# Transposed weight copies in pieces, the gradient of k inside the inverse loop, and weight-gradient jobs filled into layer 1's backward, in a forward-and-backward kernel of two SSM-convolution and MLP layers

## The chip, the cores and the metric

The kernel runs on one core of a Trainium2 chip. The metric is the device time of one execution in microseconds (us); the kernel before takes 758.16 us, the median of three runs (757.78 to 758.56). The profile is of one execution, with a span of 748.5 us.

## The reference

Forward pass of two equal layers on a sequence of S = 2048 tokens of width D = 448, all in bf16, and the gradients of its eight inputs for a given grad_out. B is one.

```
x = q
twice:  x = x + A(layernorm(x), k, v, shift_k, ssm_k, ssm_D)
        x = x + silu(layernorm(x) @ w1) @ w2           # w1: 448x1792, w2: 1792x448
A(q, ...) : k_shift[s] = sum over t < 4 of k[s - t] * shift_k[:, t]
            kv = k_shift * v
            y  = causal convolution of kv with ssm_k over the sequence (by FFT) + kv * ssm_D
            return q * y
outputs: x, and d/dq, d/dk, d/dv, d/dshift_k, d/dssm_k, d/dssm_D, d/dw1, d/dw2
```

The convolution result y doesn't depend on x, so it is computed once and used by both layers. d/dw1 and d/dw2 are sums over both layers and all tokens.

## The kernel before, in words

One core does everything in three parts.

**Prefix** (`_ssm_prefix`, to about 100 us): the shift convolution and the FFT convolution as matmuls against constant matrices. It leaves y in SBUF (`Ysb`) and the spectra in DRAM.

**Main** (`class Main`, about 100 to 512 us): the layers in chunks of 512 tokens (c = 0 to 3). The code counts L = 0 for the first layer and L = 1 for the second. The hidden width 1792 is NF = 14 blocks of 128, in two halves of seven. In the text, "layer 1" is L = 0 and "layer 2" is L = 1.

- `h` makes one half of the hidden activations: matmuls `ps_h` (L535, in `contract`), silu into `aT` on ScalarE, a copy `dT` for the slope. `out` multiplies with w2 (`ps_o`, L652). The program overlaps `h` of the next chunk with `out` of this one.
- `aT` and `ghT` tiles share the tag T with three buffers. Each half also has to be kept for the weight gradients, which contract over tokens and so need tokens on partitions: `store_turned` (L496) transposes the half by DMA into `turned` in two pieces and, at the next call, stores it to DRAM (`A_d` for activations, `GH_d` for hidden gradients, one for each layer). These transposes and stores are all issued by SyncE, in one queue.
- `load_weights_T` (L516) makes `w2T` and `w1T`, the transposed weights for the backward pass, by three DMA transposes straight from the inputs. It is called after chunks 1 and 2 of layer 1's forward.
- The backward of a chunk is `ga` and `gn`. `ga` makes the hidden gradient: matmuls `ps_g` with `w2T`, a ScalarE copy `ghp` (L679), a VectorE product with the slope into `ghT` (L687). `gn` multiplies with `w1T` (`ps_n`, L725) and goes back through both layernorms on VectorE and ScalarE (`ln_bwd`). `hook` inserts the slopes and the transposed gradient `gT` of the next chunk; `gT` goes through PSUM tag "tr", which has two banks.
- Layer 2's backward is interleaved with its forward; layer 1's backward runs by itself, about 410 to 512 us.

**Suffix** (`_ssm_suffix`, about 512 us to the end): the backward of the convolution, woven with the weight gradients. These are 56 jobs (`_job`, L864): load one transposed block `dstat` (128 x 16 x 128) from DRAM, and contract it with a moving tensor in 16 matmuls `ps_d` (L872). For each of 14 blocks `_gw2` runs two jobs (layer 1 with `X`, which holds the gradient into layer 2 by then, and layer 2 with `GO`, the loaded grad_out) and `_gw1` two (layer 2 with `mov3`, layer 1 with `mov1`, the normalised inputs). That is 896 matmuls in all. `dstat` has five slots once the suffix's own pool is open, three before. A gradient block of w1 is turned back by DMA (`turn`, L896) before its store. `weave(n)` puts the next n job matmuls between the suffix's own: after each block of the first FFT stage, the transposes, the spectra, the inverse, the gK blocks and the inverse loop `for i in range(8)` (L1076), which makes d/dv and `gks`. After that come the reduction for shift_k, then all remaining job matmuls, and in program order last `for g in range(8)` (L1127), which forms d/dk from `gks` with four products and three sums a group on VectorE.

What sets the order: the framework takes the instructions in program order as priority, places each on its engine's queue in an order that it simulates, and inserts the semaphores. An instruction whose inputs are there early can be placed ahead of others; `issue_after(i)` keeps what is traced in its block behind i on i's engine, and `keep_in_program_order(i)` holds an instruction at its place. [...]

Of the kernel before, what the change touches and what calls it, by code (L numbers as in the profile page):

```python
# [10 lines left out]
FP32 = mybir.dt.float32  # L11
# [109 lines left out]
def kernel(  # L121
# [38 lines left out]
    k.AP_d = dram.tile([4, P, S], BF16, name="AP_d")  # L160
    k.GH_d = [dram.tile([P, NF, NT, P], BF16, name=f"GH_d{i}") for i in range(2)]

# [318 lines left out]
class Main:  # L481

    def __init__(self, k, es):
        self.k, self.nc, self.tc = k, k.nc, k.tc
        nc, tc = k.nc, k.tc
        pool = lambda name, **kw: es.enter_context(tc.tile_pool(name=name, bufs=1, reuse_waits="tile", **kw))
        self.wt = pool("mwt")
        self.w2T = self.wt.tile([P, ND, F], BF16, name="w2T")
        self.w1T = self.wt.tile([P, NF, D], BF16, name="w1T")
        self.td = pool("mtd")  # L490
        self.ch = pool("mch")
        self.X = k.X
        self.late = None
        self.w1sb, self.w2sb, self.Y = k.w1sb, k.w2sb, k.Ysb

    def store_turned(self, dst, tile_, c, hh, groups=((0, 4), (4, 7))):  # L496
        nc = self.nc
        self.flush()
        an = self.td.tile([P, NF // 2, 4, P], BF16, name="turned", tag="S", bufs=2)
        for lo, hi in groups:  # L500
            nc.sync.dma_start_transpose(out=an[:, lo:hi].rearrange("p a t f -> p (a t) f"), in_=tile_[:, lo:hi, :].rearrange("p a s -> p (a s)"))
        lo, hi = groups[0][0], groups[-1][1]
        self.late = lambda: nc.sync.dma_start(out=dst[:, 7 * hh + lo:7 * hh + hi, 4 * c:4 * c + 4, :], in_=an[:, lo:hi])
# [6 lines left out]
    def turn_plain(self, i):  # L510
# [3 lines left out]
        self.late = lambda: self.nc.sync.dma_start(out=self.k.A_d[0][:, W2_PLAIN[i]], in_=an[:])  # L514

    def load_weights_T(self, which):  # L516
        nc, k = self.nc, self.k
        if which == 1:
            nc.sync.dma_start_transpose(out=self.w1T[:], in_=k.B_w1)
            return  # L520
        nc.sync.dma_start_transpose(out=self.w2T[:, 0:3, :], in_=k.B_w2[:, 0:384])
        nc.sync.dma_start_transpose(out=self.w2T[:, 3:4, :], in_=k.B_w2[:, 320:448])

# [147 lines left out]
    def ga(self, c, L, gT, dT, mid=None, loads=(None, None)):  # L671
        nc, k = self.nc, self.k
        ld = []
        ghT = [self.td.tile([P, NF // 2, 512], BF16, name=f"ghT{h}", tag="T", bufs=3) for h in range(2)]
        for fp in range(NF // 2):
            ps = k.psum.tile([P, 2, 512], FP32, name="ps_g", tag="mm", bufs=2)
            self.contract(ps, self.w2T, gT, 2 * fp, 2, None if fp == 6 else (fp + 1) % 2)
            gh = self.ch.tile([P, 2, 512], BF16, name="ghp", tag="ghp", bufs=2)
            k.last_gh = nc.scalar.copy(gh[:], ps[:])  # L679
            k.bal.add("act", 0.95)  # L680
            k.bal.add("dve", -0.5)
            if mid:
                with self.tc.issue_after(k.last_gh.ins):
                    mid(fp)
            for u in ((0, 1),) if fp != 3 else ((0,), (1,)):
                hh, o = divmod(2 * fp + u[0], 7)
                nc.vector.tensor_tensor(out=ghT[hh][:, o:o + len(u), :], in0=dT[hh][1][:, o:o + len(u), :], in1=gh[:, u[0]:u[0] + len(u), :], op=ALU.mult)  # L687
            k.bal.add("dve", 1.2)
            if fp in (3, 6):
                hh = (fp - 3) // 3  # L690
                if loads[hh]:
                    ld.append(self.load_d(*loads[hh]))
                self.store_turned(k.GH_d[L], ghT[hh], c, hh)
        return (ghT, *ld) if ld else ghT
# [20 lines left out]
    def gn(self, c, L, ghT, nb, gres, na, hook=None):  # L715
# [5 lines left out]
        for tl in range(4):  # L721
# [6 lines left out]
            k.bal.add("act", 0.75)  # L728
            k.pe_engine = mm.ins.engine
            if hook:  # L730
                hook(tl, mm.ins, last_u.ins)
# [35 lines left out]
    def run(self):  # L767
# [17 lines left out]
        for c in range(4):  # L785
# [7 lines left out]
            nT = self.b_tr(nb)  # L793
            if c in (1, 2):
                self.load_weights_T(3 - c)
            fol = []
# [3 lines left out]
        for c in range(4):  # L800
# [27 lines left out]
            self.gn(c, 1, ghT, nb, lambda tl: gb[:, tl, :], na, None if c < 3 else hook(0, d1))  # L828
            na, nb = na1, nb1
        for c in range(4):  # L830
            dT, (nb, na), (gb, gT) = ((None, d0), (None, d1)), nl, box.pop()
            ghT = self.ga(c, 0, gT, dT, (lambda fp: self.slope(e0, {1: (0,), 2: (1,), 4: (2,), 5: (3,)}.get(fp, ()))) if c < 3 else None, ((c + 1, 1) if c < 3 else None, (c + 2, 0) if c < 2 else None))
            if c < 3:
                d0, (ghT, d1, *e) = e0, ghT
                e0 = e[0] if e else None
            self.gn(c, 0, ghT, nb, lambda tl: self.X[:, 4 * c + tl, :], na, hook(c + 1, d1) if c < 3 else None)
            if c < 3:
# [26 lines left out]
def _job(k, ps, src, ft, mov, slot, start, stop, first=None):  # L864
    pl, tag, bufs = slot
    st = pl.tile([P, NT, P], BF16, name="dstat", tag=tag, bufs=bufs)
    with ExitStack() as es:
        if first is not None:
            es.enter_context(k.tc.issue_after(first))
        k.job_load = k.nc.sync.dma_start(out=st[:], in_=src[:, ft, :, :]).ins  # L870
    for t in range(NT):
# [17 lines left out]
def _gw1(k, pool, slots):  # L889
# [6 lines left out]
    def turn(ft, o):  # L896
        if ft < NF - 2:
            o7 = pool.tile([P, ND, P], BF16, name="do7", tag="do7", bufs=2)
            nc.sync.dma_start_transpose(out=o7[:, 0:3, :], in_=o[:, 0:384])
            nc.sync.dma_start_transpose(out=o7[:, 3:4, :], in_=o[:, 320:448])  # L900
            nc.gpsimd.dma_start(out=out7w[:, :, ft * P:(ft + 1) * P], in_=o7[:, 0:3, :])
            nc.gpsimd.dma_start(out=k.outs[7][384:448, ft * P:(ft + 1) * P], in_=o7[64:128, 3, :])
            return
# [8 lines left out]
    for ft in range(NF):  # L912
        ps = psum.tile([P, 512], FP32, name="ps_d", tag="tr", bufs=2)
        for L, mov in ((1, k.mov3), (0, mov1)):
            slot = slots.pop(0)
            slots.append(slot)
            for n, i in enumerate(_job(k, ps, k.GH_d[L], ft, mov, slot, L == 1, L == 0)):
                if hold and n == 7:
                    turn(*hold)
                    hold = None  # L920
                yield i
        o = pool.tile([P, D], BF16, name="dout", tag="dout", bufs=2)
        nc.scalar.copy(o[:], ps[:, :D])  # L923
        hold = (ft, o)
# [3 lines left out]
def _ssm_suffix(k):  # L928
# [7 lines left out]
    with ExitStack() as es:  # L936
# [6 lines left out]
        def jobs():  # L943
            yield from _gw2(k, k.dp, range(1), [(k.dp, "dstat", 3)], first=k.go_jobs.ins)
            yield from _gw2(k, k.dp, range(1, NF), both)
            yield from _gw1(k, dp2, both)
# [14 lines left out]
        for n2 in range(16):  # L961
            with _in_turn(k):
                _fft_stage1(k, n2, k.gYb[:, n2, :], A1, psum, nc.scalar if n2 < 12 else None)
            weave(4 if n2 < 12 else 12)
        with tc.tile_pool(name="sspec2", bufs=1, reuse_waits="tile") as p1:
# [105 lines left out]
        nc.gpsimd.dma_start(out=k.outs[6].rearrange("(o d) -> o d", o=1), in_=gD[:])  # L1071

        out3_pm = _pm(k.outs[3][0])
# [52 lines left out]
        weave(2 * NF * 2 * NT)  # L1126
        for g in range(8):  # L1127
            acc = p2.tile([P, 2, D], FP32, name="gk_acc", tag="gK", bufs=4)
            gk = p2.tile([P, 2, D], BF16, name="gk", tag="gk", bufs=2)
            last = None  # L1130
            for j in range(4):
                pj = p2.tile([P, 2, D], BF16, name="gkp", tag="gkv", bufs=2)
                for u, n in ((0, 2),) if 2 * g + j != J - 1 else ((0, 1), (1, 1)):
                    r = 2 * g + j + u
                    src = gks[:, r:r + n, :] if r < J else gkh[:, r - J:r - J + n, :]
                    nc.vector.tensor_tensor(out=pj[:, u:u + n, :], in0=src, in1=skb[:, j, :].unsqueeze(1).to_broadcast([P, n, D]), op=ALU.mult)
                if last is not None:
                    nc.vector.tensor_tensor(out=gk[:] if j == 3 else acc[:], in0=last[:], in1=pj[:], op=ALU.add)
                    last = acc
                else:  # L1140
                    last = pj
            nc.gpsimd.dma_start(out=out2_pm[:, 2 * g:2 * g + 2, :], in_=gk[:])

# [29 lines left out]
```

## Time and profile before

| what | value |
|---|---|
| time, three runs | 758.16 us (757.78 to 758.56) |
| span of the profile | 748.5 us |
| busy: TensorE / VectorE / ScalarE / GpSimd | 696.3 / 506.1 / 438.3 / 108.9 us |
| DMA | 184.88 MB moved, 247 GB/s mean |
| ps_d matmuls (all jobs) | 896, all of them in the suffix |
| turned<-ghT, transposes | 32, median 6.3 us from issue to landing |
| turned<-aT, transposes | 28, median 5.8 us |
| dstat<-GH_d, loads of 512 KB | 28, median 4.5 us |

TensorE is busy 93% of the span, so what counts is where it is not. In the lists of the profile a line gives the kernel line, the engine, the operation, and what is written from what. A releaser after an arrow is what ended a wait. "SPq" is SyncE's queue: the time of a row there is that of generating the transfer's descriptors, not of moving its bytes.

### The profile page before, as it was taken

Reading aid. Unit: us, or ns where it says so; the run is one execution under the profiler, and the core shown is the slowest. Engines: PE = TensorE matmul, PEld = TensorE weight load, DVE = VectorE, ACT = ScalarE, POOL = GpSimd, SP = SyncE. Lnnn points to the kernel's source line nnn. Section 1 sums busy time; section 2 is a strip of 40 time slices with the busy share of each in tenths; the row PEclk is TensorE's granted clock in tenths of the full one; section 3 lists DMA queues with packets and bytes.
Section 4 is the critical chain, followed back from the end, with each engine's and each line's share of the span. In section 5 each row is a group of like instructions: output and inputs, shape, how many; then the busy total and the mean of one; then the engine's idle time right before and its main releaser. Section 6 shows DMA issues by size and latency. Waiting matters only on the chain.

```text
span 748.5 us, 12463 instructions
## 1 busy us (share of the span) xinstructions
PE 696.3 (93%) x4836; PEld 370.4 (49%) x4881; DVE 506.1 (68%) x1059; ACT 438.3 (59%) x555; POOL 108.9 (15%) x180
## 2 busy tenths in 40 slices
PE   5988789599999999999999998989999999999997
PEld 5766533244444444443444334434556767555553
DVE  4878878468833398795966997899208773426970
ACT  4688767266636848688585787866325675410001
POOL 1143222022200000001000000000201112313321
PEclk9999999889999999999999999999999999999999
DMA  9979999999987889996989999999996976977993
GB/s 290 249 178 275 350 242 291 189 274 260 251 217 204 217 198 244 200 221 162 190 222 236 276 312 275 265 266 255 331 270 219 373 268 237 343 243 220 251 249 68
DMA packets 208343, 184.88 MB, mean 247 GB/s; under 512 B 155739, under 2 KB 184479, under 8 KB 207133
## 3 DMA queue, kind: packets, MB, share of 16 engines
q1 hardware_dynamic: 194272, 127.39, 68.9%
q0 software_dynamic: 13088, 54.18, 21.1%
q10 hardware_dynamic: 924, 2.52, 1.0%
q8 instruction: 38, 0.62, 0.4%
q14 instruction: 21, 0.16, 0.1%
HBM read 76.66 MB, written 65.87 MB: 190 GB/s over the span
## 4 chain that ended last, share of the span: by engine, by line
PE 53%; DVE 21%; ACT 10%; DMA 9%; issue 4%; POOL 1%; SPq 0%; DVEq 0%; ACTq 0%; POOLq 0%
PE ps_d L872 22%; PE ps_h L535 9%; PE ps_o L652 7%; DMA KB<-Z 3%; PE ps_n L725 3%; DVE lb_junk L700 3%; DMA turned<-aT 2%; PE ps_g L535 2%; DVE dT L113 2%; DVE lb_u L711 2%; DVE ghT L687 2%; PE ps_v L233 2%; PE ps_v L234 2%; DMA K_sb<-in_A_ssm_k_dram 2%; DVE lb_u L741 2%
## 5 line engine op out<-in xcount | busy, mean ns | idle before, releaser
L872 PEld LDWEIGHTS <-dstat 128*128 128x128 bf16 x896 | 85.5, 98 | 74.9 <-issue 0.2
L535 PE MATMUL ps_h<-nT,w1sb 128*128 128x512 bf16 (+1 forms) x432 | 103.9, 388 | 13.7 <-DVE dT L113 10.4
L535 PE MATMUL ps_g<-gT,w2T 128*128 128x512 bf16 (+1 forms) x432 | 93.3, 380 | 7.4 <-ACT ghp L679 6.0
L725 PE MATMUL ps_n<-w1T,ghT 128*128 128x448 bf16 x448 | 89.8, 353 | 2.8 <-DVE ghT L687 1.9
L627 ACT ACTIVATE aT<-ps_h 128x1024 bf16<-128x1024 f32 (+1 forms) x64 | 58.6, 917 | 56.0 <-PE ps_h L535 37.8
L652 PE MATMUL ps_o<-w2sb,aT 128*128 128x448 bf16 x448 | 91.3, 354 | 0.0
L872 PE MATMUL ps_d<-mov,dstat 128*128 128x448 bf16 x448 | 86.6, 352 | 0.0
L113 DVE CAST dT<-ps_h 128x1024 bf16<-128x1024 f32 (+1 forms) x55 | 58.4, 1064 | 40.8 <-ACT aT L627 40.7
L535 PEld LDWEIGHTS <-w1sb 128*128 128x128 bf16 (+1 forms) x448 | 36.5, 97 | 76.5 <-issue 49.2
L535 PEld LDWEIGHTS <-w2T 128*128 128x128 bf16 (+1 forms) x448 | 34.9, 97 | 65.5 <-issue 33.0
L679 ACT CAST ghp<-ps_g 128x1024 bf16<-128x1024 f32 x56 | 55.5, 1007 | 17.4 <-PE ps_g L535 12.7
L725 PEld LDWEIGHTS <-ghT 128*128 128x128 bf16 x448 | 42.3, 98 | 45.0 <-DVE ghT L687 5.1
L652 PEld LDWEIGHTS <-aT 128*128 128x128 bf16 x448 | 42.0, 98 | 42.8 <-issue 5.4
L923 ACT CAST dout<-ps_d 128x448 bf16<-128x448 f32 x14 | 7.5, 532 | 77.8 <-PE ps_d L872 77.8
L872 PE MATMUL ps_d<-GO,dstat 128*128 128x448 bf16 x224 | 49.7, 352 | 0.2
L872 PE MATMUL ps_d<-X,dstat 128*128 128x448 bf16 x224 | 49.6, 352 | 0.1
L727 ACT ACTIVATE lb_u<-ps_n,rstd 128x448 f32<-128x448 f32 x32 | 20.3, 636 | 31.1 <-DVE X L712 15.4
L234 PEld LDWEIGHTS <-pb 128*128 128x128 bf16 x336 | 32.5, 98 | 9.2 <-DVE pb L453 5.8
L233 PEld LDWEIGHTS <-pa 128*128 128x128 bf16 x336 | 32.8, 98 | 7.2 <-DVE pa L452 4.3
L687 DVE TENSOR_TENSOR ghT<-dT,ghp 128x1024 bf16<-128x1024 bf16 (+1 forms) x32 | 19.5, 620 | 20.9 <-ACT ghp L679 20.8
L612 ACT ACTIVATE dTl<-dTl 128x1024 bf16<-128x1024 bf16 (+1 forms) x32 | 29.8, 947 | 3.4 <-DMA dTl<-DT_d 3.4
L653 DVE TENSOR_TENSOR X<-X,ps_o 128x448 bf16<-128x448 bf16 x32 | 19.7, 617 | 15.3 <-PE ps_o L652 15.1
(205 smaller groups left out, 1170.0 us busy)
## 6 DMA issues: line engine op xcount, KB each, us to landing
GH_d<-turned SPq DMA_DIRECT2D x16, 896.0 KB, 4.9
dstat<-A_d SPq DMA_DIRECT2D x28, 512.0 KB, 5.7
dstat<-GH_d SPq DMA_DIRECT2D x28, 512.0 KB, 4.5
A_d<-turned SPq DMA_DIRECT2D x12, 896.0 KB, 5.1
DT_d<-dT POOLq DMA_DIRECT2D x8, 896.0 KB, 7.4
dTl<-DT_d SPq DMA_DIRECT2D x8, 896.0 KB, 6.1
spec_K<-Z POOLq DMA_DIRECT2D x7, 512.0 KB, 8.5
KB<-Z POOLq DMA_DIRECT2D x14, 256.0 KB, 12.1
```

What stands on the lines that cost most here:

```text
L113: eng.tensor_copy(out, in_)
L233: nc.tensor.matmul(o, lhsT=pa[:, i * P:(i + 1) * P], rhs=k.Gsb[:, ga, :], start=True, stop=False)
L234: nc.tensor.matmul(o, lhsT=pb[:, i * P:(i + 1) * P], rhs=k.Gsb[:, gb, :], start=False, stop=True)
L535: self.nc.tensor.matmul(ps[:, u, :], lhsT=w[lo:hi, b, f:f + P], rhs=x[lo:hi, b, :], start=(seen[u] == 1), stop=(seen[u] == ND))
L612: self.k.last_slope = self.nc.scalar.activation(s, s, ACT.Derivative_silu)
L627: last = nc.scalar.activation(a, ps[:, 0:n, :], ACT.Silu)
L652: nc.tensor.matmul(po[:, :D], lhsT=aT[ft // 7][0][:, ft % 7, tl * P:(tl + 1) * P], rhs=self.w2sb[:, ft, :], start=(ft == 0), stop=(ft == N ...
L679: k.last_gh = nc.scalar.copy(gh[:], ps[:])
L687: nc.vector.tensor_tensor(out=ghT[hh][:, o:o + len(u), :], in0=dT[hh][1][:, o:o + len(u), :], in1=gh[:, u[0]:u[0] + len(u), :], op=ALU.mult)
L700: nc.vector.scalar_tensor_tensor(out=junk[:], in0=u0, scalar=1.0, in1=n_t, op0=ALU.mult, op1=ALU.mult, accum_out=cp[:, 1:2])
L725: mm = nc.tensor.matmul(pn[:, :D], lhsT=ghT[ft // 7][:, ft % 7, tl * P:(tl + 1) * P], rhs=self.w1T[:, ft, :], start=(ft == 0), stop=(ft == ...
L872: i = k.nc.tensor.matmul(ps[:, :D], lhsT=st[:, t, :], rhs=mov[:, t, :], start=start and t == 0, stop=stop and t == NT - 1)
```

## The change

Four things are changed.

1. The transposed weights are fetched in six pieces instead of three transposes: after the third call of `store_turned`, each further call also issues one piece behind its own transposes, held at its place.
2. The first two blocks of `_gw2` (four jobs, 64 matmuls) can be consumed inside layer 1's backward: `fill(n)` takes up to n job matmuls and puts them behind TensorE's latest instruction, one or two after each group of `ps_g` (not in chunk 0) and two after each tile of `ps_n`. What is left of the two blocks is taken first in the suffix.
3. Layer 1's hidden gradient isn't transposed when it is made. GpSimd stores it plain (`GP_d`), and each layer-1 job of `_gw1` loads its block by a DMA transpose from DRAM. The gradient blocks of w1 are padded to 512 columns, so that `turn` needs one transpose instead of two.
4. d/dk: groups 0 to 5 are computed inside the inverse loop (`grad_k(i - 2)`), the last two after the jobs. To go with it, `weave` gives 4 instead of 12 matmuls in the last four FFT blocks, and 34 instead of 4 from the fourth turn of the inverse loop on.

```diff
@@ Main.__init__ / store_turned / load_weights_T
+        self.turns = 0
+        self.pieces = [(self.w2T[:, a:b, :], k.B_w2[:, lo:hi]) for a, b, lo, hi in ((0, 2, 0, 256), (2, 3, 256, 384), (3, 4, 320, 448))]
+        self.pieces += [(self.w1T[:, a:b, :], k.B_w1[:, a * P:b * P]) for a, b in ((0, 5), (5, 10), (10, NF))]
...
             nc.sync.dma_start_transpose(out=an[:, lo:hi].rearrange("p a t f -> p (a t) f"), in_=tile_[:, lo:hi, :].rearrange("p a s -> p (a s)"))
+        self.turns += 1
+        if self.turns > 3 and self.pieces:
+            out, src = self.pieces.pop(0)
+            i = nc.sync.dma_start_transpose(out=out, in_=src)
+            self.tc.keep_in_program_order(i)
...
-    def load_weights_T(self, which):
-        nc, k = self.nc, self.k
-        if which == 1:
-            nc.sync.dma_start_transpose(out=self.w1T[:], in_=k.B_w1)
-            return
-        nc.sync.dma_start_transpose(out=self.w2T[:, 0:3, :], in_=k.B_w2[:, 0:384])
-        nc.sync.dma_start_transpose(out=self.w2T[:, 3:4, :], in_=k.B_w2[:, 320:448])
...
-            if c in (1, 2):
-                self.load_weights_T(3 - c)
@@ Main.ga / gn
+            if L == 0:
+                self.fill(1 if fp else 2)
             k.last_gh = nc.scalar.copy(gh[:], ps[:])
...
-                self.store_turned(k.GH_d[L], ghT[hh], c, hh)
+                if L == 1:
+                    self.store_turned(k.GH_d, ghT[hh], c, hh)
+                else:
+                    self.flush()
+                    nc.gpsimd.dma_start(out=k.GP_d[7 * hh:7 * hh + 7, :, 512 * c:512 * (c + 1)].rearrange("ft f s -> f ft s"), in_=ghT[hh][:])
...
             k.pe_engine = mm.ins.engine
+            if L == 0:
+                self.fill(2)
@@ Main.run
+        k.jobs = _gw2(k, k.dp, range(2), [(k.dp, "dstat", 3)], first=k.go_jobs.ins)
+        bb = nc.cur_bb.bb
+
+        def fill(n):
+            last = next(i for i in reversed(bb.instructions) if i.engine == k.pe_engine)
+            with self.tc.issue_after(last):
+                for _ in zip(range(n), k.jobs):
+                    pass
+
         for c in range(4):
+            self.fill = (lambda n: None) if c == 0 else fill
...
+            self.fill = fill
             self.gn(c, 0, ghT, nb, lambda tl: self.X[:, 4 * c + tl, :], na, hook(c + 1, d1) if c < 3 else None)
@@ _job
-        k.job_load = k.nc.sync.dma_start(out=st[:], in_=src[:, ft, :, :]).ins
+        if src is None:
+            k.job_load = k.nc.sync.dma_start_transpose(out=st[:], in_=k.GP_d[ft]).ins
+        else:
+            k.job_load = k.nc.sync.dma_start(out=st[:], in_=src[:, ft, :, :]).ins
@@ _gw1
-            nc.sync.dma_start_transpose(out=o7[:, 0:3, :], in_=o[:, 0:384])
-            nc.sync.dma_start_transpose(out=o7[:, 3:4, :], in_=o[:, 320:448])
+            nc.sync.dma_start_transpose(out=o7[:], in_=o[:])
...
-            for n, i in enumerate(_job(k, ps, k.GH_d[L], ft, mov, slot, L == 1, L == 0)):
+            for n, i in enumerate(_job(k, ps, k.GH_d if L == 1 else None, ft, mov, slot, L == 1, L == 0)):
...
-        o = pool.tile([P, D], BF16, name="dout", tag="dout", bufs=2)
-        nc.scalar.copy(o[:], ps[:, :D])
+        o = pool.tile([P, 512], BF16, name="dout", tag="dout", bufs=2)
+        nc.gpsimd.memset(o[:, D:], 0.0)
+        nc.scalar.copy(o[:, :D], ps[:, :D])
@@ _ssm_suffix
-            yield from _gw2(k, k.dp, range(1), [(k.dp, "dstat", 3)], first=k.go_jobs.ins)
-            yield from _gw2(k, k.dp, range(1, NF), both)
+            yield from k.jobs
+            yield from _gw2(k, k.dp, range(2, NF), both)
...
-            weave(4 if n2 < 12 else 12)
+            weave(4)
...
+        def grad_k(g):
...
-            weave(4)
+            weave(4 if i < 3 else 34)
...
+            if i > 1:
+                grad_k(i - 2)
...
         weave(2 * NF * 2 * NT)
-        for g in range(8):
...
+        for g in range(6, 8):
+            grad_k(g)
```

`grad_k(g)` has the body of the old loop over g, unchanged.

More of the change, by code (lines that the diff above doesn't have):

```diff
@@ L160 @@
     k.AP_d = dram.tile([4, P, S], BF16, name="AP_d")
-    k.GH_d = [dram.tile([P, NF, NT, P], BF16, name=f"GH_d{i}") for i in range(2)]
+    k.GH_d = dram.tile([P, NF, NT, P], BF16, name="GH_d")
+    k.GP_d = dram.tile([NF, P, S], BF16, name="GP_d")
     bf = mybir.dt.np(BF16)
@@ L898, in turn @@
             o7 = pool.tile([P, ND, P], BF16, name="do7", tag="do7", bufs=2)
-            nc.sync.dma_start_transpose(out=o7[:, 0:3, :], in_=o[:, 0:384])
-            nc.sync.dma_start_transpose(out=o7[:, 3:4, :], in_=o[:, 320:448])
+            nc.sync.dma_start_transpose(out=o7[:], in_=o[:])
             nc.gpsimd.dma_start(out=out7w[:, :, ft * P:(ft + 1) * P], in_=o7[:, 0:3, :])
-            nc.gpsimd.dma_start(out=k.outs[7][384:448, ft * P:(ft + 1) * P], in_=o7[64:128, 3, :])
+            nc.gpsimd.dma_start(out=k.outs[7][384:448, ft * P:(ft + 1) * P], in_=o7[0:64, 3, :])
             return
@@ L1071, in _ssm_suffix @@
         nc.gpsimd.dma_start(out=k.outs[6].rearrange("(o d) -> o d", o=1), in_=gD[:])
+        def grad_k(g):
+            acc = p2.tile([P, 2, D], FP32, name="gk_acc", tag="gK", bufs=4)
+            gk = p2.tile([P, 2, D], BF16, name="gk", tag="gk", bufs=2)
+            last = None
+            for j in range(4):
+                pj = p2.tile([P, 2, D], BF16, name="gkp", tag="gkv", bufs=2)
+                for u, n in ((0, 2),) if 2 * g + j != J - 1 else ((0, 1), (1, 1)):
+                    r = 2 * g + j + u
+                    src = gks[:, r:r + n, :] if r < J else gkh[:, r - J:r - J + n, :]
+                    nc.vector.tensor_tensor(out=pj[:, u:u + n, :], in0=src, in1=skb[:, j, :].unsqueeze(1).to_broadcast([P, n, D]), op=ALU.mult)
+                if last is not None:
+                    nc.vector.tensor_tensor(out=gk[:] if j == 3 else acc[:], in0=last[:], in1=pj[:], op=ALU.add)
+                    last = acc
+                else:
+                    last = pj
+            nc.gpsimd.dma_start(out=out2_pm[:, 2 * g:2 * g + 2, :], in_=gk[:])
         out3_pm = _pm(k.outs[3][0])
@@ L1126, in _ssm_suffix @@
         weave(2 * NF * 2 * NT)
-        for g in range(8):
[L1128 to L1142, printed above, removed]
+        for g in range(6, 8):
+            grad_k(g)
 _INS = ['A_q', 'A_k', 'A_v', 'A_shift_k', 'A_ssm_k', 'A_ssm_D', 'B_x', 'B_w1', 'B_w2', 'grad_out']
```

## The prediction

> **What bounds the kernel now.** I read the page's slices first, then busy time by stage, then what ended TensorE's idle time in the stages where there is any.
>
> ```profile
> PE   5988789599999999999999998989999999999997
> DVE  4878878468833398795966997899208773426970
> PEclk9999999889999999999999999999999999999999
> ```
>
> Each digit is a fortieth of the span (18.7 us). TensorE is at 9 nearly everywhere after the prefix; the one hole is its 5 in slice 8 (131 to 150 us), with the granted clock at 8 beside it. Busy time by stage (TensorE, its weight loads, VectorE, ScalarE, GpSimd; then clock, DMA share, GB/s):
>
> ```profile
> 100.00:150.00 50.00, 37.38 (x185) 15.06 (x190) 33.23 (x79) 26.36 (x34) 10.10 (x14) 0.90 1.07 221
> 398.00:512.00 114.00, 105.43 (x564) 47.81 (x572) 100.02 (x274) 80.21 (x115) 2.17 (x4) 1.00 1.07 274
> 512.00:640.00 128.00, 126.81 (x1090) 81.19 (x1094) 66.69 (x130) 71.36 (x83) 20.38 (x36) 1.00 0.85 283
> 640.00:749.00 109.00, 103.86 (x774) 55.00 (x772) 57.06 (x93) 17.73 (x27) 28.29 (x48) 0.99 0.77 223
> ```
>
> The suffix (512 on) is TensorE itself: 1.2 us idle up to 640, then full until 744. Time can be won only from the 12.6 us idle in the first row and the 8.6 us in the second, since no matmul disappears. The hole, on TensorE and on SyncE's queue:
>
> ```profile
> 136.33 2.85 PE L535 MATMUL ps_h<-nT,w1sb 128*128 128x512 bf16 x11
> 148.44 3.29 PE L535 MATMUL ps_h<-nT,w1sb 64*128 64x512 bf16 x8 [9.26 <-DVE dT L113]
> ```
>
> ```profile
> 101.47 10.12 SPq L521 DMA_TRANSPOSE w2T<-in_B_w_dram  x1
> 111.64 2.45 SPq L522 DMA_TRANSPOSE w2T<-in_B_w_dram  x1
> 114.14 10.42 SPq L519 DMA_TRANSPOSE w1T<-in_B_w_dram  x1
> 124.66 13.19 SPq L501 DMA_TRANSPOSE turned<-aT  x2
> 147.02 0.38 SPq L503 DMA_DIRECT2D A_d<-turned  x1
> ```
>
> SyncE generates the weights' three transposes without a break from 101.5 to 124.6. The first turn of an activation tile aT queues behind them and lands at 147. ScalarE then waits 14.2 us "DMA turned<-aT" for that slot (tag T, three buffers), and TensorE stands for 9.26 us. In the second row TensorE's idle time is spread (410 to 512 us; after the bar: busy, mean ns, idle before and what ended it):
>
> ```profile
> L535 PE MATMUL ps_g<-gT,w2T 128*128 128x512 bf16 (+1 forms) x216 | 47.2, 380 | 5.7 <-ACT ghp L679 4.8
> L725 PE MATMUL ps_n<-w1T,ghT 128*128 128x448 bf16 x226 | 45.8, 353 | 2.8 <-DVE ghT L687 1.9 <-ACT lb_u L727 0.7
> ```
>
> 8.5 us in some twenty short waits for ScalarE and VectorE: room for matmuls that wait for neither.
>
> **What the Trainium skill says.** "Perfetto Trace Analysis", What "DMA-bound" means, lists the issuing sequencer as a bound of its own, solid slices being descriptor generation; the five rows above are that case. "TensorE: Matmul & The Clock Gate", HAM oscillation, says that a TensorE gap over about 3.4 us brings the throttle back. The trace agrees: the clock is 0.65 from 147 to 157 us, and in the backward of layer 1, whose gaps are at most 1.0 us, it is 1.00. "PSUM — Partial Sum Buffer", Engine vs sequencer instructions, has matmuls start in program order; so a filled job whose load is late stops everything behind it.
>
> **Part 1, weights in pieces.** Removed: three transposes with 23.0 us of issue ahead of the first turn. Added: the same bytes in six pieces, one behind each of turns 4 to 9, so 2.5 to 6.7 us each (10.12 us x 256/384 columns for the largest; 10.42 x 5/14 = 3.7 for one of w1T). Turns 1 to 3 have nothing ahead of them. Behind a piece in SyncE's queue stand the late store of that turn and the next turns. Between 150 and 235 us a half's two transposes and store take about 5 us of SyncE's time in some 18 us, so a piece fits; and aT comes round only after three halves, so several us more of landing reach nobody. The last piece follows turn 9 (about 228 to 233 us), and w1T is first read after 250. Gain: the 9.26 us, plus the cold restart. Eight ps_h matmuls took 3.29 us against 1.72 in "323.16 1.72 PE ps_h L535 x8" of the chain, sixteen transposes 1.91 against 1.06, five ps_o 1.46 against about 1.1: 2.7 us. Sum **12.0 us**. From 150 to 250 TensorE is busy 98.4 of 100 us, so nothing slower lies under the hole. Bounds 8 (another small wait in its place) and 12.5.
>
> **Part 2, w2 jobs filled in.** Fills: gn 4 chunks x 4 tiles x 2 = 32, ga 3 chunks x 8 = 24 (chunk 0 has none), 56 matmuls. A job of 16 takes 3.03 us in the chain (189 ns each): 10.6 us leave the TensorE-bound suffix and enter a stage with 8.5 us idle. If they displaced only busy time the gain would be 0; if they filled every hole, 8.5. Those in ga stand just where ps_g waits for ghp, those in gn where TensorE is ahead of VectorE anyway. I take 5. Their waits: dstat of the first jobs was loaded at 409.7, and X is complete when gn of layer 2 ends. GO is first read by fill 17, in gn of chunk 1 (about 447 us); it was issued at 438.6 and takes 8.6, and in the new kernel it has fewer transposes ahead of it. ps_d now holds one of the two "tr" banks, so a gradient's second transpose must wait for the copy of the first: three times up to 1 us, where the order has other matmuls to put between. Counted in the 5.
>
> **Part 3, layer 1's gradient unturned.** Sixteen SBUF transposes of ghT leave SyncE in 410 to 512, and GpSimd writes ghT plain. The same kind of store exists (AP_d<-aT, 5.7 us to landing, where a turn took 6.3), so ghT's slot is free no later: 0. Instead 14 loads become transposes out of DRAM in the last 100 us. The same form stands in the trace of before (the page has 5.6 us to landing for it; duration ns min/median/max here):
>
> ```profile
> L513 SPq DMA_TRANSPOSE turned<-AP_d x4: 2257/2418/2863, 230.4 to 288.8; - x4
> ```
>
> A load is issued when the job five before it ends, four jobs or 12.4 us ahead: hidden. SyncE's queue in one gw1 step of before:
>
> ```profile
> 701.81 1.20 SPq L899 DMA_TRANSPOSE do<-dout  x1
> 703.06 1.23 SPq L900 DMA_TRANSPOSE do<-dout  x1
> 704.39 3.19 SPq L870 DMA_DIRECT2D dstat<-GH_d  x2
> 707.87 1.46 SPq L899 DMA_TRANSPOSE do<-dout  x1
> ```
>
> A step is 6.06 us; SyncE's own work in it becomes one do transpose (1.2 to 2.5), one turned load (2.4) and one plain (0.4, the rest of the 3.19 being waits): 4.0 to 5.3 us. It holds, with little to spare. The padding memset on GpSimd is one small instruction per step, behind stores that end well within the step: 0.
>
> **Part 4, gradient of k in the loop; weaves 4 for 12 and 34 for 4.** One group costs VectorE four products and three sums:
>
> ```profile
> L1136 DVE TENSOR_TENSOR gkp<-gks,skb 128x896 bf16<-128x896 bf16 (+1 forms) x30 | 17.1, 605 | 2.4 <-DMA out_dram<-gsk 2.2
> L1138 DVE TENSOR_TENSOR gk_acc<-gkp 128x896 f32<-128x896 bf16 x8 | 8.7, 1092 | 0.3
> ```
>
> 4 x 0.605 + 3 x 1.09 = 5.7 us, with the loop's own two products (0.6 each) 6.9 us a turn. TensorE has 34 x 0.189 + 4 x 0.19 = 7.2 us a turn: VectorE stays just ahead, and ScalarE's gkv copy, which now shares its two buffers with the products, has the last product and sum (1.7 us) to pass in. Before, these groups lay under 67 us of jobs, so moving them gains nothing by itself. It keeps them off the end: jobs left after the shift reductions are 896 - 56 - 666 = 174 (33 us) instead of 348. The cost is in mov1: its load needs X, which gw2 now gives up in the middle of the gK section, and it is first read 33 matmuls later. By the counts that is about 11.8 us with the gK blocks between, against 9.4 us for the load: 0 to 3 us of stall. For this and for dense loads in the loop (DMA share 0.96 in 640 to 660 already) I take **1.5 us** loss.
>
> **Sum.** 758.2 - 12.0 - 5.0 + 1.5 = 742.7; I say 742.5.
>
> **Rivals.** (a) The fills only displace busy matmuls, or the transposes on one bank give it back: 758.2 - 12.0 + 1.5 = 747.7. For: VectorE is busy 91 of 102 us there. Against: the waits are on single copies, which a matmul in between covers. 0.20. (b) Everything hides: 758.2 - 12.0 - 8.5 = 737.7. For: TensorE ran dense through 640 to 740. Against: a fill cannot meet every wait in a fixed order. 0.12. (c) The pieces hold up later turns, and half of the hole opens again around 165 to 200 us: 742.5 + 6 to 10 = about 750. For: DMA share is about 1.0 there. Against: three halves of slack. 0.10. (d) The other side: turned loads cost SyncE as much in the last stage as the turns of ghT did under load. Sixteen of those took 68 us of issue from 416 to 512 (4.25 us for 448 KB, so 4.9 for 512 KB). A step is then 4.9 + 0.4 + 2 = 7.3 us against 6.06, 14 x 1.3 = 18 us, and 742.5 + 18 = 760.5. For: the kind is the same. Against: the AP_d row read from DRAM at 2.4 us. 0.08. The forecast has 0.50.
>
> **Range.** 737 to 753 holds the forecast, (a), (b) and (c); out are (d) and a tenth for a bound missed. Faster 0.89, within 0.2% 0.03, slower 0.08.
>
> **What would show it.** No TensorE gap over 2 us and clock near 1.0 from 100 to 250 us (part 1). In layer 1's backward, TensorE idle down from 8.5 to about 3 us, the stage about 5.5 us longer, with 56 ps_d matmuls in it (part 2). No ghT turn in it, and turned loads of 2 to 3 us issue later, TensorE dense from there to the end (part 3). gkp and gk_acc inside the inverse loop with no TensorE wait on gkv, and at most 3 us before the first matmul on mov1 (part 4). The prediction is wrong if ps_d waits for dstat, GO or mov1, or if aT still waits for a turn.

## The result, and the profile after

The changed kernel takes 747.5 us (median of four runs, 738.98 to 755.04) against 758.36 us for the kernel before (four runs, 757.78 to 759.94). By executions within 1.5% of the fastest of their kernel alone, the ratio is 0.975 (95% interval 0.9721 to 0.978); since one and the same kernel here differs by more than that through a wait of its own, which the experiments below show, medians and means over all executions are used from here on.

The predicted time was 742.5 us, in a range of 737 to 753. The four executions are two pairs, 739.0 and 740.4 us, 754.6 and 755.0 us; the median stands between them, where no execution was. The profiled execution has a span of 753.2 us. The slices of its page that answer to those shown of before:

```profile
PE   6988789999569999999999999999999999999997
DVE  4878878788423379696785997797516776299150
PEclk9999989999879999999999999999999999999999
```

The hole hasn't gone. It has moved from slice 8 to slices 11 and 12, 188 to 226 us, and the clock dips with it (0.54 of full speed from 200 to 210 us). Here is the timeline of TensorE around it in the kernel after:

```profile
196.34 1.79 PE L536 MATMUL ps_h<-nT,w1sb 64*128 64x512 bf16 x8
212.98 3.26 PE L536 MATMUL ps_h<-nT,w1sb 128*128 128x512 bf16 x8 [14.85 <-DVE dT L113]
```

SyncE's queue ahead of it (start, duration of the row):

```profile
165.88 10.12 SPq L505 DMA_TRANSPOSE turned<-aT  x2
176.04 10.44 SPq L509 DMA_TRANSPOSE w2T<-in_B_w_dram  x1
187.21 19.36 SPq L505 DMA_TRANSPOSE turned<-aT  x1
206.62 3.51 SPq L509 DMA_TRANSPOSE w2T<-in_B_w_dram  x1
```

A single turn of aT took 19.4 us of issue and the piece before it, a quarter of w2T, 10.4 us. ScalarE waited 15.7 us for that turn. In another execution of the same program, profiled in the experiments (span 740.3 us), the same four entries read:

```profile
157.23 8.16 SPq L505 DMA_TRANSPOSE turned<-aT  x2
165.43 2.42 SPq L509 DMA_TRANSPOSE w2T<-in_B_w_dram  x1
170.31 4.09 SPq L505 DMA_TRANSPOSE turned<-aT  x1
174.45 4.07 SPq L509 DMA_TRANSPOSE w2T<-in_B_w_dram  x1
```

and TensorE has no gap over 0.5 us between 106 and 300 us. The same instructions in the same order can cost 0 or 15 us.

The time of a row in SyncE's queue therefore isn't that of generating descriptors alone, as it was described ahead. The rows of w1T's transpose in the kernel before (114.14 us in its first profile, 111.97 in the second, shown below) take 10.42 and 19.39 us, and transpose packets of 1.64 and 1.58 MB begin in them; w1T is 1.61 MB. In these rows SyncE's queue goes on only at the pace at which the packets move.

Busy time by stage in that second execution: layer 1's forward up to the first ps_g, layer 2, layer 1's backward, the suffix up to the gK blocks, the rest (columns as in the table of stages in the prediction).

```profile
105.10:228.30 123.20, 120.46 (x630) 53.28 (x640) 86.59 (x176) 79.65 (x98) 22.75 (x30) 1.00 1.04 262
228.30:399.30 171.00, 165.25 (x883) 74.53 (x897) 125.42 (x276) 121.28 (x156) 7.17 (x10) 1.00 0.86 211
399.30:508.50 109.20, 104.65 (x545) 47.06 (x551) 93.40 (x257) 74.84 (x106) 10.65 (x15) 1.00 0.65 227
508.50:620.30 111.80, 109.85 (x929) 69.74 (x934) 66.20 (x126) 63.83 (x73) 18.45 (x32) 1.00 0.79 261
620.30:740.30 120.00, 111.06 (x878) 60.95 (x876) 57.80 (x94) 24.02 (x34) 31.52 (x62) 1.00 0.98 226
```

For the first profile of before the same five stages are 135.7, 171.0, 101.8, 116.8 and 119.7 us. The first stage is 12.5 us shorter. Layer 1's backward is 7.4 us longer, for 10.6 us of jobs moved into it. Suffix and end together are only 4.7 us shorter, where those jobs' 10.6 us are missing. So in these two traces parts 2 to 4 cost 2.7 us on balance. (The prefix, which wasn't changed, is 1.6 us longer in the second.)

### The profile page after: what moved, and what is told of

The parts are those of the page before. It is cut to its first block, busy times and chain, and to the rows that moved or that the text cites. A ratio compares the mean times of both kernels' runs of the same rounds, so it can differ in the third digit from the quotient of the medians.

```text
span 753.2 us, 12492 instructions
## 1 busy us (share of the span) xinstructions
PE 701.6 (93%) x4881; PEld 370.2 (49%) x4881; DVE 508.4 (67%) x1059; ACT 438.3 (58%) x555; POOL 118.4 (16%) x202
## 4 chain that ended last, share of the span: by engine, by line
PE 56%; DVE 20%; ACT 10%; DMA 8%; issue 4%; POOL 1%; SPq 0%; ACTq 0%; DVEq 0%; POOLq 0%
PE ps_d L893 20%; PE ps_h L536 9%; PE ps_o L653 7%; PE ps_g L536 5%; PE ps_n L732 4%; DMA KB<-Z 3%; DMA turned<-aT 3%; DVE lb_junk L707 3%; DVE lb_u L718 2%; DVE dT L113 2%; ACT nb L280 2%; PE ps_v L234 2%; PE ps_v L235 2%; DMA K_sb<-in_A_ssm_k_dram 2%; DVE lb_u L750 1%
## 5 line engine op out<-in xcount | busy, mean ns | idle before, releaser
L536 PE MATMUL ps_h<-nT,w1sb 128*128 128x512 bf16 (+1 forms) x448 | 106.9, 393 | 18.1 <-DVE dT L113 16.4
L536 PE MATMUL ps_g<-gT,w2T 128*128 128x512 bf16 (+1 forms) x448 | 96.0, 381 | 3.2 <-ACT ghp L682 2.7
L893 PE MATMUL ps_d<-X,dstat 128*128 128x448 bf16 x224 | 53.2, 353 | 0.0
L893 PE MATMUL ps_d<-GO,dstat 128*128 128x448 bf16 x224 | 51.7, 353 | 0.0
## 6 DMA issues: line engine op xcount, KB each, us to landing
GP_d<-ghT POOLq DMA_DIRECT2D x8, 896.0 KB, 10.1
```

Source lines behind the costliest of these rows:

```text
L536: self.nc.tensor.matmul(ps[:, u, :], lhsT=w[lo:hi, b, f:f + P], rhs=x[lo:hi, b, :], start=(seen[u] == 1), stop=(seen[u] == ND))
L893: i = k.nc.tensor.matmul(ps[:, :D], lhsT=st[:, t, :], rhs=mov[:, t, :], start=start and t == 0, stop=stop and t == NT - 1)
```

## The experiments

The runs are in three batches, each on one chip, with the kernel before beside them: 39, 7 and 75 executions of it.

### One size of hole, or many?

Theory A: the hole has a fixed size, set by what stands ahead in SyncE's queue. Theory B: the transposes are slowed by what else the DMA engines carry, so the size varies. Both kernels ran again unchanged.

> The kernel before, unchanged, profiled a second time. In its first profile TensorE stood 9.26 us at 139 us behind a late turn of aT, and that profile's span (748.5 us) was about 7 us under what the timed runs (758 us) would give. Theory A (the hole has one size, set by the 23 us of weight transposes ahead in SyncE's queue): again 9 to 10 us. Theory B (the turns and weight transposes are slowed by whatever else the DMA engines carry at that moment, so that the hole varies from execution to execution): another size, perhaps 16 us, with the same instructions everywhere else.

> The changed kernel, unchanged, profiled again. Its first profile had a hole of 14.85 us at 198 us behind a turn that took 19.4 us to issue. Theory A (pieces remove the wait, the first profile was a disturbed execution): no hole over 2 us before 250 us, 738 to 740 us. Theory B (the forward of layer 1 is close to what the transposing DMA can do beside the stores of GpSimd, so a late turn comes and goes): a hole of some other size, and timed runs in two groups about 15 us apart.

The kernel before, beside these runs: 735.4 to 775.7 us in 39 executions, median 752.0; in four more, one of them profiled, 752.5 to 760.8. Its new profile shows the hole in the same place, nearly twice as long as the first time (timeline of TensorE):

```profile
134.94 2.85 PE L535 MATMUL ps_h<-nT,w1sb 128*128 128x512 bf16 x11
155.51 3.29 PE L535 MATMUL ps_h<-nT,w1sb 64*128 64x512 bf16 x8 [17.71 <-DVE dT L113]
```

and on SyncE w1T's transpose took 19.4 us where it had taken 10.4:

```profile
111.97 19.39 SPq L519 DMA_TRANSPOSE w1T<-in_B_w_dram  x1
131.46 20.63 SPq L501 DMA_TRANSPOSE turned<-aT  x2
```

The changed kernel: 735.5 to 754.8 us in 12 executions, median 742.7. Eight are at 743.5 or below, four at 751 or above. The size varies, as theory B has it; whether its cause is the right one, these two runs don't show.

### Part 1 alone, and everything but part 1

```diff
 # part 1 alone: the kernel before, and
+        self.turns += 1
+        if self.turns > 3 and self.pieces: ...
-            if c in (1, 2):
-                self.load_weights_T(3 - c)
...
 # all but part 1: the changed kernel with these lines the other way round
```

> The kernel before with part 1 alone: weights in six pieces behind turns 4 to 9, nothing else changed. If part 1 carries most of the gain, as predicted (12.0 us of 15.5): about 12 us or more under before, 741 to 746 us. If the fills carry it: within 5 us of before.

> The changed kernel with the weights' three transposes as before: parts 2 to 4 without part 1. Predicted 5.0 - 1.5 = 3.5 us under before, about 754.5 us; the two traces so far show 1.9 us from the start of layer 1's backward to the end (TensorE's last matmul 6.5 us later at the start of it and 4.6 us later at the end), so 756 us. If the pieces are worth little: about 742 us.

Part 1 alone: median 740.0 us (20 executions, 735.7 to 755.6), 12.0 below the kernel before in the same batch (10.1 by the means, within 4.4, twice the standard error). All but part 1: median 751.4 (12 executions, 738.2 to 761.8), 0.6 below it. So part 1 carries the gain. It is a gain in how often and how long the hole appears, not in the best time: the fastest executions are 735.4 us (before), 735.5 (changed) and 735.7 (part 1 alone), and six of the 20 are still at 746.7 or above. The profiled execution of part 1 alone has a hole of 2.70 us, that of all but part 1 one of 4.34 us.

### What makes a transpose late

Three changes to the kernel before, with one suspect altered in each. With plain loads the backward multiplies with untransposed weights, so that its gradients are not those of the reference; the bytes are as many.

```diff
 # plain loads in place of the weights' transposes
-            nc.sync.dma_start_transpose(out=self.w1T[:], in_=k.B_w1)
+            nc.sync.dma_start(out=self.w1T[:], in_=k.B_w2.rearrange("(c p) d -> p c d", p=P))
...
 # stores on SyncE (or, in the third, on ScalarE: nc.scalar)
-            nc.gpsimd.dma_start(out=k.DT_d[c, half], in_=dT[:])
+            nc.sync.dma_start(out=k.DT_d[c, half], in_=dT[:])
...
-                nc.gpsimd.dma_start(out=k.AP_d[:, :, 512 * c:512 * (c + 1)]...
+                nc.sync.dma_start(out=k.AP_d[:, :, 512 * c:512 * (c + 1)]...
```

> The kernel before, with the three weight transposes replaced by plain loads of as many bytes into the same tiles, at the same place in the queue (so the backward multiplies with untransposed weights and the gradients are not those of the reference; no work is left out). The kernel before has a hole of 0 to 25 us behind the first turn of aT, and 735 to 776 us over its executions on this chip. Theory A (the transposes of the weights, ahead in the queue and slow beside other transfers, make the hole): no hole in the forward of layer 1, all executions at 735 to 739 us. Theory B (the turns of aT are slowed by the stores of GpSimd whatever is in front): the scatter stays, a median of 745 us or more.

> The kernel before, with the stores of dT and of the plain part of aT in layer 1's forward issued by SyncE, in the queue of the transposes, in place of GpSimd. Theory A (weights alone are to blame): hole and scatter as before, median about 752 us. Theory C (transposes are slow because packets of GpSimd's queue and of SyncE's alternate on the DMA engines): packets of one queue only, the transposes at about 20 ns a packet again, no hole, 735 to 740 us. If SyncE's own order gets in the way: a hole of a fixed size.

> The same stores issued by ScalarE, so a third hardware queue and not GpSimd's software queue. Theory C (any second queue's packets between the transposes make them slow): hole and scatter as before, about 752 us. Theory D (it is the software queue[...] that makes engines stand): no hole, 735 to 741 us. ScalarE gets eight or twelve issues of some 0.5 us, so up to 2 us more where it is the bound.

| kernel | executions | median us | range us |
|---|---|---|---|
| before, in this batch | 7 | 757.5 | 750.4 to 766.5 |
| plain weight loads | 4 | 738.8 | 735.7 to 745.1 |
| stores on SyncE | 4 | 741.0 | 740.5 to 741.5 |
| stores on ScalarE | 4 | 748.1 | 744.0 to 755.8 |

Without the weights' transposes the large hole goes; some scatter remains, against the expectation. With the stores in the transposes' own queue it goes too, as theory C has it, although the three weight transposes are still ahead. Their rows are then 8.72, 3.49 and 7.18 us long (10.12, 2.45 and 10.42 in the first profile of before), and the first turn lands in time:

```profile
112.98 7.18 SPq L519 DMA_TRANSPOSE w1T<-in_B_w_dram  x1
120.26 3.68 SPq L501 DMA_TRANSPOSE turned<-aT  x1
124.05 0.52 SPq L638 DMA_DIRECT2D DT_d<-dT  x1
124.66 2.83 SPq L501 DMA_TRANSPOSE turned<-aT  x1
```

With the stores in ScalarE's queue, which the profile lists as hardware_dynamic where GpSimd's is software_dynamic, the hole is there, though smaller (2.42 us in the profiled execution, the fastest of the four; a scatter of 12 us). So in these runs the long hole comes only with both: the weights' transposes queued ahead of the turn, and these stores in another queue beside them. It isn't a matter of GpSimd's software queue alone (theory D).

The packets show the slowing. I counted the 256-byte packets of SyncE's transposes from 100 to 240 us, in stretches of 1 us with and without packets of 512 bytes and more of another queue under way, as KB moved a microsecond in the stretches that had any. "Alone" means without another queue; SyncE's own plain packets stand in some of these stretches:

```
                          beside another queue   alone    hole in that execution
before, first profile              83             167         9.26 us
before, again                      68             164        17.71
after, first profile               50             169        14.85
after, again                      101             175         none
part 1 alone                       69             169         2.70
all but part 1                     78             163         4.34
stores on SyncE                    92             167         none over 1.1
stores on ScalarE                  80             163         2.42
plain weight loads                 78             161         none over 1.1
```

Alone, transposes move 161 to 175 KB/us in every execution. Beside another queue they move 50 to 101, and this number differs between executions of the same program. It doesn't by itself give the size of the hole: 68 KB/us goes with 17.71 us, and 69 with 2.70. The single packet's mean goes from 21 to 25 ns alone to 26 to 49 ns beside; single ones of 1 us and more are among both.

A rival is that the stores merely take their share of the DMA engines. On average they do: in the stretches beside another queue all queues together move 204 to 278 KB/us, and in the others 191 to 218. But in the wait itself both queues are slow. From 184 to 196 us of the first profile of after, the transposes move 27 and the other queues 50 KB/us, with packets of 136 and 805 ns in the mean. In the row of w1T's transpose in the first profile of before (114.14 to 124.56 us), which also has other queues' packets beside it, they move 158 and 121 KB/us, with packets of 23 and 284 ns. So sharing alone doesn't make the long holes. The Trainium skill, "DMA: Bandwidth & Descriptors", Queues, rings and completion order, says that a DMA engine goes round the queues that it has work for, packet by packet. That fits the sharing, but which engine stands for what isn't in these traces, nor why the loss differs from one execution to the next; both stay open.

### The fills alone

```diff
-            self.fill = (lambda n: None) if c == 0 else fill
+            self.fill = lambda n: None
...
-            self.fill = fill
```

> The changed kernel with no job matmuls in layer 1's backward; parts 1, 3 and 4 stay. From the end of layer 2's backward to the last gradient matmul, layer 1's backward takes 101.6 us before and 109.15 us after, with 10.6 us of jobs in it. If the fills are what lengthens it: 101 to 101.6 us here, less if the missing turns of ghT had slowed it (part 3 worth something, under 100.5). The rest of the span, 227 to 232 us with the fills, should be 10.6 us longer, so 238 to 242 us, where before has 236.4: what is above 236.4 is the price of parts 3 and 4 in the last stage.

There is one execution of this variant. Layer 1's backward is 100.6 us, as in the second profile of before (100.6; the first had 101.8). So the ghT turns that left it had cost nothing, and the fills lengthen it by 8.5 us. The second half of the expectation came to nothing. From the last gradient matmul to the end it is 257.1 us, where 238 to 242 were expected. In SyncE's queue:

```profile
516.34 26.87 SPq L991 DMA_TRANSPOSE Zg<-A1g  x2
```

A plain load behind these two transposes made TensorE wait 13.16 us, and mov1 another 3.17. In the 27 us the transposes moved 25 KB/us and other queues 102. It looks like the same fault at another place, so the last stage can't be read from this run.

### Parts 2 to 4 with the scatter taken down

The stores of dT and aT were now on SyncE in all four kernels: part 1 alone; the changed kernel; the changed kernel with part 3 undone (but for the padding); the changed kernel with part 4 undone (but for the weave of 4 in the last FFT blocks).

```diff
 # part 3 undone
-                if L == 1:
-                    self.store_turned(k.GH_d, ghT[hh], c, hh)
-                else: ...
+                self.store_turned(k.GH_d[L], ghT[hh], c, hh)
...
 # part 4 undone
-            weave(4 if i < 3 else 34)
+            weave(4)
-            if i > 1:
-                grad_k(i - 2)
...
-        for g in range(6, 8):
+        for g in range(8):
```

> The kernel before with part 1 alone, and layer 1's stores of dT and of the plain part of aT issued by SyncE. Part 1 alone gave 735.7 to 755.6 us, with a hole in some executions; the stores on SyncE alone gave 740.5 to 741.5 us, with 3.7 us of small waits left in the forward (126.9 us against 123.2 without any). If the collision of two queues is what makes transposes late: no scatter, 736 to 739 us. If the pieces have a hole of their own from another cause: executions up to 750 us still.

> The changed kernel with those two stores issued by SyncE. If the collision is the cause of its two groups (735 to 743 and 751 to 755 us): one group, about 737 to 742 us. What parts 2 to 4 are worth is then the difference to the run with part 1 alone: predicted 3.5 us faster; by the traces so far (layer 1's backward 8.5 us longer for 10.6 us of jobs moved, the last stage 4.5 to 9 us shorter) 2 us faster to 4 us slower.

> As the run before, with part 3 undone: layer 1's hidden gradient turned in SBUF and stored turned, its jobs load plainly (the single padded transpose of the w1 gradient stays). If the turned loads out of DRAM, slowed by GpSimd's stores, are the price in the last stage: no wait of ps_d for dstat, from the last gradient matmul of layer 1's backward to the end 226 to 228 us where the changed kernel had 227 to 232, and 2 to 5 us faster in all than the run before. If part 3 helps layer 1's backward: that stage over 110 us instead of 109.15.

> The changed kernel with the two stores on SyncE and part 4 undone: the gradient of k after all jobs in program order, weave 4 in the inverse loop. If the dense loop with its stores of d/dk is what slows the turned loads and holds ps_sk: the waits of 0.8 us for dstat and of 2.3 us at ps_sk go, 2 to 4 us faster than with part 4. If moving it is needed: with 56 jobs fewer at the end VectorE's 45 us of groups still lie under some 60 us of jobs, so no time is lost at the end either way.

Each of the four had 22 executions, with the kernel before beside them at a median of 754.8 us (75 executions, 735.8 to 774.6):

| kernel, stores on SyncE | mean us | standard deviation | largest | last ps_n to the end, profiled execution |
|---|---|---|---|---|
| part 1 alone | 742.8 | 2.6 | 750.3 | 236.2 |
| changed | 743.3 | 2.5 | 747.4 | 232.4 |
| part 3 undone | 740.3 | 1.9 | 743.9 | 227.8 |
| part 4 undone | 741.2 | 2.0 | 746.2 | 229.4 |

Part 1 alone scattered by 6.7 us with the stores on GpSimd (in another batch, on another chip) and by 2.6 us here, with the same mean (742.8), where 736 to 739 us and no scatter were expected. The long holes go, but for one execution of 750.3 us that wasn't profiled, and some 5 us of small waits in the forward come for them (128.3 us from the first ps_h to the first ps_g, against 123.2 in the second profile of after). Against part 1 alone, parts 2 to 4 together are 0.5 us slower, within 1.5 us (twice the standard error). Part 3 costs 3.0 us, within 1.3, and part 4 2.2 us, within 1.4, each beside all the others. If these differences simply added up, part 2 would be worth 4.7 us (3.0 + 2.2 - 0.5); no run has part 2 alone, so this isn't shown. Why the last stage is longer is in part in SyncE's queue. In the changed kernel with the stores on SyncE, in the gK section and at the start of the inverse loop:

```profile
628.63 0.32 SPq L915 DMA_DIRECT2D mov<-N_d  x1
629.05 10.14 SPq L889 DMA_TRANSPOSE dstat<-GP_d  x1
640.97 10.47 SPq L889 DMA_TRANSPOSE dstat<-GP_d  x1
```

where GpSimd's stores of gK and of d/dv run beside. TensorE then waits 1.76 us for mov1 and 0.87 us for a turned load:

```profile
642.13 0.92 PE L893 MATMUL ps_d<-mov,dstat 128*128 128x448 bf16 x4 [1.76 <-DMA mov<-N_d]
```

With part 3 undone the loads in this stretch are plain and all quick, and no ps_d waits (duration ns min/median/max):

```profile
L886 SPq DMA_DIRECT2D dstat<-GH_d x26: 319/322/397, 622.2 to 717.3; - x26
```

A further 1.6 to 2.3 us stand at the reduction for shift_k (ps_sk) in four of the six traces that have the turned loads, and not with part 3 undone. The profile names no releaser for them. They stay with part 4 undone (1.65 us), so the dense loop isn't their cause, against the expectation. In that trace no ps_d waits, although a turned load took 11.9 us there too. What the waits of ps_sk are stays open, and so does how much of the 3.0 and 2.2 us is theirs.

The version with part 3 undone and the stores on SyncE has the lowest mean of all kernels run, apart from the one with plain weight loads. Its median is 740.0 us, against 742.7 for the changed kernel and 752.0 for the kernel before in the batch where these two ran, and 754.8 for the kernel before in its own batch.

## Why the prediction was right or wrong

**Part 1 (12.0 us): the size came out by luck, the reason was half right.** Part 1 alone is 12.0 us faster by the medians, 10.1 by the means (752.9 to 742.8). But the 12.0 us were read from a single draw of a hole that measured 9.26 us there and 17.71 us in the next profile. The cold restart, priced at 2.7 us, holds: in the second profile of before the first stage is 20.6 us longer than without a hole (143.8 against 123.2), 17.7 of it the hole, so 2.9. What failed is the step "turns 1 to 3 have nothing ahead of them ... so several us more of landing reach nobody". It took the hole of 9.26 us as a constant of the program and the queue's order as its cause. The traces show a wait of 0 to 18 us, drawn anew in each execution by how badly the transposes fare beside another queue's stores (why they fare differently stays open). A piece keeps SyncE busy for 2.4 or for 10.4 us, and the turn behind it for 4 or for 19. Three halves of slack are enough for the first pair and not for the second. Rival (c), given 0.10, is what happened in the profiled execution, with a larger hole than it allowed, and by their times in four of the next twelve, which weren't profiled. The sign was there in the trace of before: two turns of 13.19 us of issue, where others took some 5, with no issue ahead of them any more.

**Part 2 (5 us): right mechanism, mis-sized.** The idle time of TensorE in layer 1's backward falls from 7.3 us (second profile of before: 100.6 us, 93.3 busy) to 4.6 us, as its waits show (idle before, and what ended it, in the second profile of before and then of after):

```profile
L535 PE MATMUL ps_g<-gT,w2T 128*128 128x512 bf16 (+1 forms) x216 | 47.2, 380 | 5.3 <-ACT ghp L679 4.4
L725 PE MATMUL ps_n<-w1T,ghT 128*128 128x448 bf16 x224 | 45.1, 353 | 2.1 <-DVE ghT L687 1.9
```

```profile
L536 PE MATMUL ps_g<-gT,w2T 128*128 128x512 bf16 (+1 forms) x216 | 48.2, 381 | 2.6 <-ACT ghp L682 1.9
L732 PE MATMUL ps_n<-w1T,ghT 128*128 128x448 bf16 x225 | 46.4, 353 | 0.9 <-DVE ghT L690 0.9
L547 PE MATMUL ps_t<-ident,X 128*128 128x128 bf16 x48 | 3.6, 219 | 1.1 <-ACT gT L111 1.1
```

The waits of ps_g and ps_n fell from 7.4 us to 3.5, not far from the 5 us that were predicted. But 1.1 us came back at the transposed gradient, which now has a single PSUM bank; the prediction had counted on other matmuls between. The stage grew by 7.4 to 8.5 us where 5.6 was predicted. For 10.6 us moved that is a gain of 2.1 to 3.2 us.

**Parts 3 and 4 (1.5 us of loss): too small.** By the count the end should be 236.4 - 10.6 = 225.8 us long. It was 227.4 and 231.9 us in the two traces of the changed kernel, and 232.4 with the stores on SyncE: a price of 1.6 to 6.6 us. The wait for mov1, bounded at 0 to 3 us, was 0 to 1.8 (3.17 in the run without fills). VectorE's turn in the loop, priced at 6.9 us against 7.2 for TensorE, took 6.6 against 7.2 (once 8.5, waiting for a store of d/dk) and never held it. What failed is "a load is issued when the job five before it ends ... hidden", with its 2.4 us of issue for a turned load. It was 2.0 to 12.2 us in the second profile of after (duration ns min/median/max):

```profile
L889 SPq DMA_TRANSPOSE dstat<-GP_d x13: 2026/3255/12164, 628.2 to 720.1; - x13
```

That price was read from AP_d loads with little beside them, and carried over into a stretch full of GpSimd's stores. Rival (d) named this effect and made it too big: 18 us against about 3.

**The sum.** Predicted: 15.7 us down to 742.5. Measured: 10.9 us by the first medians, 9.2 in the first batch of experiments. That the median there, 742.7, falls on the predicted 742.5 is luck too: the gain is 6.5 us smaller than predicted, and the kernel before starts 6.2 us lower, at 752.0. Part 1 brings all of it, and parts 2 to 4 give back 0.5 us, within 1.5, where 3.5 us of gain were expected.

## What to carry to other kernels

A wait seen in one trace is one draw: before pricing its removal, profile the same program again, and ask whether the transfer behind it took as long as its peers. In this kernel DMA transposes moved best with no other queue beside them, and their rows in the issuing queue lasted as long as their packets; stores put into the same queue took the long waits away, at the price of small ones. Matmuls filled into an engine's short waits gain what those waits were, less what the fill's own PSUM bank and late loads give back.

## What the hardware showed that I hadn't expected

Transposes of 256-byte packets ran at 161 to 175 KB/us without another queue, stretches that they filled only in part included (290 KB/us over 5 us at best, with the stores on SyncE), and at 50 to 101 KB/us beside packets of another queue. The loss differed between executions of one program, and in the long waits the other queue was slow as well. There were 40 us between the fastest and the slowest of 39 executions of the kernel before (735.4 to 775.7). The holes that were profiled account for up to 20.6 us of that, restart included; what the slowest executions lost, and where, wasn't seen. In the traces the clock's dip follows the hole: it falls to half speed 4.5 us after the first hole of before begins and rises 5.5 us after it ends (2.6 and 4.8 us in the first profile of after). A hole of 2.42 us (stores on ScalarE), shorter than the 3.4 us that the prediction names, was followed by 3.4 us at half speed; one of 2.70 us (part 1 alone) was not. Slow transposes came up in three places, each with another queue's packets beside them: the forward of layer 1, the Zg transposes (26.9 us of issue for two in one run), and the turned loads at the end.
